# Decayed linear attention and two fp32 feed-forward layers on one core: preparing four instead of two weight pairs of the second layer in the first layer's middle blocks, and four instead of six in its last block

## The chip, the cores and the metric

One core of one Trainium2 chip runs the whole program. The metric is the device time of one execution in microseconds (us), as the median of several runs. A change of this kernel under 0.2% (2.3 us) can't be told from no change.

## The reference

```python
# attention: B, H, S, D = 4, 8, 768, 64
for t in range(S):
    state = gamma * state + outer(k[t], v[t])        # per batch and head
    y[t] = (1/sqrt(D)) * q[t] @ state
x = y.transpose(0, 2, 1, 3).reshape(3072, 512)
# first layer, w_in 512 x 2048, w_out 2048 x 512
h = x @ w_in;  x = max(0.01*h, h) @ w_out
# second layer, the same shapes
h = x @ w_in;  out = (h * cos(h)) @ w_out
```

All of it is in fp32.

## The kernel before

**Precision.** An fp32 operand is split into a high part, rounded to TensorE's fp32r format, and a low part, the remainder. `mm3` (L364 to L366) makes one product of three matmuls: high by high, low by high, high by low. Every operand needs a cast (ScalarE, called ACT in the profile) and a subtraction (VectorE, called DVE, or GpSimd, called POOL).

**Stages.** The 3072 tokens are six blocks of 512. In the first layer the 2048 inner columns are 16 tiles of 128, one iteration each: `gemm1` (12 matmuls into a PSUM tile `hp`), the leaky activation on ACT (L562), the cast of its result `g` (ACT, L570), the low part of `g` (DVE, L574, in `low_g`), and `gemm2_a` (12 matmuls into four banks `acc`) two iterations later. The attention of the next block is done in slots between these: per unit of 128 tokens and four heads the keys and queries are split (`prep_qk`: casts L454 and L458 on ACT, subtractions L459 on DVE and L462 on POOL), then come the scores on TensorE (PE) with the mask on DVE (L491), and for two units at a time the products with the values (L504 to L519) and their evacuation (L530 and L539 on DVE, L541 on ACT, L542 on POOL). The last block has no attention beside it.

**Second layer.** It starts when the first has ended, and multiplies pairs of 256 x 256 blocks by Strassen's scheme in seven products (`product`, "P1" to "P7"). Its weights must be prepared ahead: `w_out` tile by tile (`half`, L650), 16 halves, and `w_in` two tiles at a time (`pair_at`, L665), eight pairs. The inputs of the first two blocks are prepared too (`xprep`, L300). Whatever is prepared goes to DRAM (`w2d`, `w2i`) and is loaded later.

**What a half and a pair are.** The weights come as 64-bit words. One tile goes through these steps: `fetch2` (L250), a DMA on SyncE's queue (SP) into the raw buffer; `exponent` (L121 and L123), two ACT instructions; `clamp`, `fraction` and `top_bits` (L126, L129, L134) on DVE; `round_up` (L139) on POOL; a cast (L271) on ACT; a low part (L278) on POOL or DVE; and the sending of both. A pair does the first steps for two tiles t1 and t2, splits three parts in 512 columns and one in 256, and forms four sums of 256 columns on DVE (`pair_sums`, L288). The raw buffer in the middle blocks is one, `cbuf[0:2]`, so the next fetch there waits for the round_up before it. The last block has its own pool with three buffers each (`last_pairs`, L701).

**What sets the order.** Everything is written in program order, and each engine and each DMA queue works in order. `Agenda` holds lists of steps under numbers called moments; `tick` (L834) runs one moment per half iteration, once after `gemm1` and once after the activation. Moment 0 is iteration 4 of the third block; the last block has the moments 88 (LAST) to 119. `half` and `pair` put their steps at m plus fixed offsets and advance m by 4 and 11; `last_pairs` puts its six pairs at 88, 92, ... 108. A send that is told to wait goes out at the next `flush` (L238), one moment later. `stage` (L102) gives four rotating buffers `o`, which the evacuations of a finished block (L776 and L778) use as well.

Of the kernel before, what the change touches and what calls it, by code (L numbers as in the profile page):

```python
# [28 lines left out]
NF = DFF // P  # L29
# [52 lines left out]
def body(ctx: ExitStack, tc: tile.TileContext, att, w1, w2, tab, out):  # L82
    nc = tc.nc
# [18 lines left out]
    def stage(tag="o"):  # L102
        return tmp.tile([P, BLK], F32, tag=tag, name=tag, bufs=4 if tag == "o" else 2)
# [107 lines left out]
    w2i = [dpool.tile([P, WIN], F32, name=f"w2i{p}") for p in range(NF // 2)]  # L211
# [31 lines left out]
    def send(out, in_, wait):  # L243
        if wait:
            late.append((out, in_))
        else:
            nc.sync.dma_start(out=out, in_=in_)

    def fetch2(raw, f, part):
        nc.sync.dma_start(out=raw, in_=w2[f, :, part * 512 : part * 512 + 512].bitcast(I32))  # L250

    def rounding(raw, t):

        def words():
            return raw().rearrange("p (n t) -> p n t", t=2)

        return (
            lambda: exponent(words(), t()),
            lambda: (clamp(t()), fraction(t()), top_bits(words(), t())),
            lambda: round_up(words(), t()),  # L260
        )

    def parts(t, dst, lo, eng, keep, out, wait=True):


        o = []

        def high():
            n = t().shape[-1]
            o.append(out(n) if out else dst()[:, :n])  # L270
            nc.scalar.copy(out=o[0].bitcast(F32R), in_=t().bitcast(F32))  # L271
            if out:
                send(dst[:, lo : lo + n], o[0], wait)

        def low():
            n = t().shape[-1]
            w = (out(n) if keep else t().bitcast(F32)) if out else dst()[:, n:]
            eng.tensor_tensor(out=w.bitcast(F32R), in0=t().bitcast(F32), in1=o[0].bitcast(F32), op=ALU.subtract)  # L278
            if out:
                send(dst[:, lo + n : lo + 2 * n], w, wait)  # L280

        return high, low
# [7 lines left out]
    def pair_sums(t1, t2):  # L290
        a11, a12, a21, a22 = t1[:, :256], t1[:, 256:], t2[:, :256], t2[:, 256:]
        sub2(a22, a21, a22, ALU.add)
        sub2(a21, a11, a21)
        sub2(a11, a22, a11)
        sub2(a12, a12, a11)

    def done(*what):
        return lambda: made.add(what)
# [260 lines left out]
    class Leaky:  # L559
        def begin(self, hp):  # L560
            t = stage("t")
            nc.scalar.activation(out=t, in_=hp, func=AF.Prelu, alpha=0.01)  # L562
            return (t,)
# [13 lines left out]
    with tc.manual_schedule():  # L577

        with ExitStack() as pctx, ExitStack() as actx:
# [57 lines left out]
            agenda = Agenda()  # L637
            START, LAST = 4, 2 * (NF * (NB - 3) - 4)
            m, turn = 0, 0

            def own(i):
                return lambda: cbuf[:, i, :]
# [7 lines left out]
            def half(f):  # L650
                nonlocal m, turn
                t = own(2 + turn % 2)
                turn += 1
                first, mid, last = rounding(raw2, t)
                high, low = parts(t, w2d[f], 0, nc.gpsimd, False, ostage)
                for i, step in enumerate((begin(f, 1), int, first, mid, last, high, low)):
                    agenda.put(m + i, step)
                agenda.put(m + 6, done("w", f))
                m += 4

            def late_fn(fn):
                first = []
                return lambda: first[0] if first else first.append(fn()) or first[0]

            def pair_at(agenda, b, p, t1, t2, raws, fetches, times, lows, out, out2):  # L665
                r1, r2 = (rounding(raw, t) for raw, t in zip(raws, (t1, t2)))
                g1 = parts(t1, w2i[p], 0, lows[0], True, out)
                both = late_fn(partial(out, 512))
                halves = iter(range(2))

                def half_out(n):
                    return both()[:, next(halves) * 256 :][:, :256]

                g4 = parts(lambda: t2()[:, 256:], w2i[p], 3072, nc.vector, True, half_out)
                g2 = parts(t1, w2i[p], 1024, lows[1], False, out2)
                g3 = parts(t2, w2i[p], 2048, lows[2], False, out2)
                steps = (
                    fetches[0], *r1, fetches[1], *r2, *g1, *g4, lambda: pair_sums(t1(), t2()),
                    g2[0], g3[0], g2[1], g3[1],
                )  # L680
                for at, step in sorted(zip(times, steps), key=lambda x: x[0]):
                    agenda.put(b + at, step)
                agenda.put(b + max(times), done("p", p))

            def pair(p):
                nonlocal m, turn
                t1, t2 = own(2 + turn % 2), own(3 - turn % 2)
                fetches = [begin(2 * p + i, 0) for i in range(2)]
                times = (0, 2, 3, 4, 4, 6, 7, 8, 5, 6, 9, 10, 10, 11, 11, 12, 12)
                pair_at(agenda, m, p, t1, t2, (raw2, raw2), fetches, times, (nc.gpsimd, nc.gpsimd, nc.vector), ostage, ostage)  # L690
                m += 11

            for f in range(8):
                half(f)
            pair(0)
            for f in range(8, NF):
                half(f)
            pair(1)
            xprep(agenda, max(m + 3, LAST + 5), 0, nc.gpsimd)

            def last_pairs(ppool):  # L701
                def room(tag, n, dt, bufs):
                    return ppool.tile([P, n], dt, tag=tag, name=tag, bufs=bufs)

                def pout(n):
                    return room("po", 512, F32, 3)[:, :n]

                for i, p in enumerate(range(2, NF // 2)):
                    t1, t2 = late_fn(partial(room, "t1", 512, I32, 3)), late_fn(partial(room, "t2", 512, I32, 3))
                    raws = [late_fn(partial(room, "raw", 1024, I32, 3)) for _ in range(2)]  # L710
                    fetches = [lambda raw=raw, f=2 * p + j: fetch2(raw(), f, 0) for j, raw in enumerate(raws)]
                    times = (-2 if i else 0, 2, 3, 4, 1, 4, 5, 6, 5, 6, 7, 8, 8, 9, 9, 10, 10)
                    pair_at(agenda, LAST + 4 * i, p, t1, t2, raws, fetches, times, (nc.gpsimd, nc.gpsimd, nc.vector), pout, ostage)

            PRE = ('0000', '0000', '0101', '0010', '0210', '0100', '0200', '0022', 0)
            SEGMENTS = [(0, 0, SPLIT[0]), (1, 0, SPLIT[1]), (0, SPLIT[0], NF), (1, SPLIT[1], NF)] + [(n, 0, NF) for n in range(2, NB)]
# [191 lines left out]
        def finish_one():  # L908
            h, r, pair = before.pop()
            nc.vector.tensor_tensor(out=r, in0=h, in1=r, op=ALU.mult)  # L910
            return r, pair
# [21 lines left out]
        acct, sum2, g1, g2 = [], {}, {}, {}  # L933
# [66 lines left out]
        for q in range(QUADS):  # L1000
# [16 lines left out]
            a, b, c, d = (bpool.tile([P, BLK], F32, tag=x, name=x, bufs=2) for x in "abcd")  # L1017
# [28 lines left out]
        last = finish_one()  # L1046
# [37 lines left out]
```

## Time and profile before

| | before |
|---|---|
| median of 3 runs | 1166.15 us (1165.49 to 1167.23) |
| the profiled execution | 1162.35 us |
| its span | 1160.4 us |
| PE busy | 1123.9 us (97%) |
| DVE busy | 843.1 us (73%) |
| ACT busy | 525.7 us (45%) |
| POOL busy | 318.6 us (27%) |

The span runs from the first to the last instruction of the profiled execution. PE is the engine that is nearly always busy, so the time is that of its matmuls and of what it waits for. The shares are means over stages: in a stretch where another engine is busy nearly all the time, PE may wait there.

### The profile page before, as it was taken

The numbers are of one execution on the slowest core, as the hardware profiler recorded it, in microseconds if no ns is written. First come the engines' busy times: TensorE is split into PE (matmuls) and PEld (weight loads), VectorE is DVE, ScalarE is ACT, GpSimd is POOL, SyncE is SP. The second block draws the span as 40 slices with busy tenths as digits, with TensorE's granted clock in tenths as the row PEclk, the third lists the DMA queues.
The fourth block names the chain that finished last, engine by engine and source line by source line (L and its number), as shares of the span: only waits on it lengthen the run. The fifth ranks groups of instructions, "written<-read, shape, count | busy, mean of one in ns | idle before, by whom it ended". The sixth has DMA issues, their size and how long they took to land.

```text
span 1160.4 us, 15609 instructions
## 1 busy us (share of the span) xinstructions
PE 1123.9 (97%) x5584; PEld 926.5 (80%) x5584; DVE 843.1 (73%) x1299; ACT 525.7 (45%) x954; POOL 318.6 (27%) x288
## 2 busy tenths in 40 slices
PE   6989989999999999999998899999999999999998
PEld 5768778888888888888876668888888888888886
DVE  7899886345455565544599798788798897877875
ACT  5556653233344444443445355444455443444432
POOL 5687773132333444432366300000000000000000
PEclk9999999999999999999999999999999999999999
DMA  9906412222334433432669456549547457333311
GB/s 341 325 5 213 164 54 92 70 77 98 126 122 145 144 129 118 162 111 88 209 228 373 164 181 210 198 167 346 188 151 242 166 216 255 127 136 136 121 79 73
DMA packets 73804, 190.12 MB, mean 164 GB/s; under 512 B 8192, under 2 KB 12416, under 8 KB 73728
## 3 DMA queue, kind: packets, MB, share of 16 engines
q1 hardware_dynamic: 73584, 188.88, 46.6%
q8 instruction: 44, 0.72, 0.3%
q14 instruction: 32, 0.26, 0.1%
q10 hardware_dynamic: 144, 0.26, 0.1%
HBM read 136.68 MB, written 52.43 MB: 163 GB/s over the span
## 4 chain that ended last, share of the span: by engine, by line
PE 75%; DVE 14%; DMA 4%; issue 2%; POOL 2%; ACT 2%; SPq 0%; ACTq 0%; POOLq 0%; DVEq 0%
PE hp L364 9%; PE hp L366 9%; PE hp L365 9%; PE acc L364 9%; PE acc L365 9%; PE acc L366 9%; PE attB L364 4%; PE attB L365 4%; PE attB L366 4%; PE attA L364 2%; PE attA L366 2%; PE attA L365 2%; DVE cbuf L129 2%; DVE g L574 2%; DVE cbuf L134 2%
## 5 line engine op out<-in xcount | busy, mean ns | idle before, releaser
L366 PE MATMUL acc<-g,w 128*128 128x512 f32 x384 | 151.8, 395 | 7.9 <-DVE g L574 7.8
L364 PE MATMUL acc<-g,w 128*128 128x512 f32 x384 | 153.1, 399 | 2.0 <-DVE o L778 1.5
L364 PE MATMUL hp<-b,w 128*128 128x512 f32 x384 | 150.6, 392 | 4.4 <-ACT t L562 3.2
L366 PE MATMUL hp<-b,w 128*128 128x512 f32 x384 | 150.1, 391 | 1.1 <-POOL b L542 1.0
L365 PE MATMUL acc<-g,w 128*128 128x512 f32 x384 | 151.0, 393 | 0.0
L365 PE MATMUL hp<-b,w 128*128 128x512 f32 x384 | 149.6, 390 | 0.0
L922 ACT ACTIVATE r<-r,bias 128x512 f32<-128x512 f32 x96 | 69.6, 725 | 88.0 <-DVE r L921 88.0
L574 DVE TENSOR_TENSOR g<-t,g 128x512 fp32r<-128x512 f32 x91 | 89.4, 983 | 18.2 <-ACT g L570 17.6
L366 PEld LDWEIGHTS acc<-g,w 128*128 128x128 f32 x384 | 72.9, 190 | 25.8 <-DVE g L574 9.9
L364 PE MATMUL hp<-w,b 128*128 128x512 f32 x224 | 87.5, 391 | 2.9 <-ACT a L1018 2.2
L364 PEld LDWEIGHTS hp<-b,w 128*128 128x128 f32 x384 | 72.3, 188 | 20.8 <-ACT t L562 4.1
L364 PEld LDWEIGHTS acc<-g,w 128*128 128x128 f32 x384 | 72.8, 190 | 18.3 <-DVE o L778 1.9
L365 PE MATMUL hp<-w,b 128*128 128x512 f32 x224 | 87.2, 389 | 0.0
L366 PE MATMUL hp<-w,b 128*128 128x512 f32 x224 | 87.1, 389 | 0.0
L570 ACT CAST g<-t 128x512 fp32r<-128x512 f32 x96 | 59.4, 619 | 61.0 <-PE acc L366 60.3
L366 PEld LDWEIGHTS hp<-b,w 128*128 128x128 f32 x384 | 72.1, 188 | 17.5 <-POOL b L542 2.4
L365 PEld LDWEIGHTS acc<-g,w 128*128 128x128 f32 x384 | 72.8, 190 | 14.0
L365 PEld LDWEIGHTS hp<-b,w 128*128 128x128 f32 x384 | 72.1, 188 | 14.3
L365 PE MATMUL acc<-w,g 128*128 128x512 f32 x192 | 75.0, 391 | 1.1 <-DVE g L574 1.0
L366 PE MATMUL acc<-w,g 128*128 128x512 f32 x192 | 74.7, 389 | 0.0
L364 PE MATMUL acc<-w,g 128*128 128x512 f32 x192 | 74.7, 389 | 0.0
L562 ACT ACTIVATE t<-hp 128x512 f32<-128x512 f32 x96 | 56.9, 593 | 32.9 <-PE hp L366 30.4
(196 smaller groups left out, 2521.0 us busy)
## 6 DMA issues: line engine op xcount, KB each, us to landing
b<-w2i SPq DMA_DIRECT2D x60, 512.0 KB, 5.7
w<-w SPq DMA_DIRECT2D x32, 512.0 KB, 7.4
raw<-att SPq DMA_DIRECT2D x32, 512.0 KB, 4.2
w<-w2d SPq DMA_DIRECT2D x32, 512.0 KB, 7.7
w<-xq SPq DMA_DIRECT2D x28, 512.0 KB, 5.3
cbuf<-w SPq DMA_DIRECT2D x20, 512.0 KB, 4.0
xq<-o SPq DMA_DIRECT2D x40, 256.0 KB, 2.3
w<-att SPq DMA_DIRECT2D x14, 512.0 KB, 7.4
```

Of the source, the lines that this page charges most:

```text
L129: nc.vector.tensor_scalar(out=t, in0=t, scalar1=3, scalar2=LOW_BITS, op0=ALU.logical_shift_left, op1=ALU.bitwise_and)
L134: nc.vector.scalar_tensor_tensor(out=t, in0=raw[:, :, 1], scalar=SIGN_TOP, in1=t, op0=ALU.bitwise_and, op1=ALU.bitwise_or)
L364: nc.tensor.matmul(o, sh, mh, start=start, stop=False)
L365: nc.tensor.matmul(o, sl, mh, start=False, stop=False)
L366: nc.tensor.matmul(o, sh, ml, start=False, stop=stop)
L562: nc.scalar.activation(out=t, in_=hp, func=AF.Prelu, alpha=0.01)
L570: nc.scalar.copy(out=pair[:, 0], in_=g)
L574: eng.tensor_tensor(out=pair[:, 1], in0=g, in1=pair[:, 0].bitcast(F32), op=ALU.subtract)
L922: nc.scalar.activation(out=r, in_=r, func=AF.Sin, bias=bias[:, 1:2], scale=1.0)
```

## The change

A half takes three moments of the timetable instead of four: the three DVE steps and the round_up stand in one moment. A pair in the middle blocks takes nine instead of eleven, and writes the low parts of its second and third part to `o` buffers instead of over t1 and t2 (`keep`). Four halves and a pair take turns, four times, which uses 84 moments; before, eight halves and a pair came twice and used 86. So the pairs 2 and 3 move from the last block to the middle blocks; the last block's remaining four stand six moments apart instead of four. The number of instructions on DVE, ACT and POOL for a pair stays the same.

```diff
@@ half
-                for i, step in enumerate((begin(f, 1), int, first, mid, last, high, low)):
+                for i, step in zip((0, 2, 3, 3, 4, 5), (begin(f, 1), first, mid, last, high, low)):
                     agenda.put(m + i, step)
-                agenda.put(m + 6, done("w", f))
-                m += 4
+                agenda.put(m + 5, done("w", f))
+                m += 3
@@ pair_at
-            def pair_at(agenda, b, p, t1, t2, raws, fetches, times, lows, out, out2):
+            def pair_at(agenda, b, p, t1, t2, raws, fetches, times, lows, out, out2, keep=False):
...
-                g2 = parts(t1, w2i[p], 1024, lows[1], False, out2)
-                g3 = parts(t2, w2i[p], 2048, lows[2], False, out2)
+                g2 = parts(t1, w2i[p], 1024, lows[1], keep, out2)
+                g3 = parts(t2, w2i[p], 2048, lows[2], keep, out2)
@@ pair
-                times = (0, 2, 3, 4, 4, 6, 7, 8, 5, 6, 9, 10, 10, 11, 11, 12, 12)
-                pair_at(agenda, m, p, t1, t2, (raw2, raw2), fetches, times, (nc.gpsimd, nc.gpsimd, nc.vector), ostage, ostage)
-                m += 11
+                times = (0, 2, 3, 3, 3, 5, 6, 6, 4, 5, 7, 8, 8, 9, 9, 10, 10)
+                pair_at(agenda, m, p, t1, t2, (raw2, raw2), fetches, times, (nc.gpsimd, nc.gpsimd, nc.vector), ostage, ostage, True)
+                m += 9
-            for f in range(8):
-                half(f)
-            pair(0)
-            for f in range(8, NF):
-                half(f)
-            pair(1)
+            OWN = 4
+            for p in range(OWN):
+                for f in range(4 * p, 4 * p + 4):
+                    half(f)
+                pair(p)
@@ last_pairs
-                for i, p in enumerate(range(2, NF // 2)):
+                for i, p in enumerate(range(OWN, NF // 2)):
...
-                    pair_at(agenda, LAST + 4 * i, p, t1, t2, raws, fetches, times, (nc.gpsimd, nc.gpsimd, nc.vector), pout, ostage)
+                    pair_at(agenda, LAST + 6 * i, p, t1, t2, raws, fetches, times, (nc.gpsimd, nc.gpsimd, nc.vector), pout, ostage)
```

**ACT in a middle block.** The rows begin with the cast of two attention products (L541). kh and qbd are the split keys and queries of the next unit, `cbuf` the weight words, `o` their high part. Before, in any of the later middle blocks:

```order
L541 CAST b_3195<-xs 128x2x128 x2
L562 ACTIVATE t<-hp 128x512
L454 CAST kh<-raw 128x256
L458 CAST qbd<-raw 64x2x128 x2
L271 CAST o<-cbuf 128x512
L570 CAST g<-t 128x512
L121 ACTIVATE cbuf<-cbuf 128x512
L123 ACTIVATE cbuf<-cbuf 128x512
L562 ACTIVATE t<-hp 128x512
L570 CAST g<-t 128x512
L454 CAST kh<-raw 128x256
L458 CAST qbd<-raw 64x2x128 x2
```

In the change, in one of the cycles whose products come just ahead of an exponent:

```order
L541 CAST b_2318<-xs 128x2x128 x2
L121 ACTIVATE cbuf<-cbuf 128x512
L123 ACTIVATE cbuf<-cbuf 128x512
L562 ACTIVATE t<-hp 128x512
L454 CAST kh<-raw 128x256
L458 CAST qbd<-raw 64x2x128 x2
L570 CAST g<-t 128x512
L271 CAST o<-cbuf 128x512
L562 ACTIVATE t<-hp 128x512
L121 ACTIVATE cbuf<-cbuf 128x512
L123 ACTIVATE cbuf<-cbuf 128x512
L570 CAST g<-t 128x512
```

The exponent (L121, L123) of a third half now stands ahead of the first unit's casts (L454, L458), and another stands ahead of the second unit's, which follow directly behind the last row shown.

**DVE in the last block.** Each row L574 is the low part of one iteration's g; the t_ tiles are the words of the pairs, `po` is an output buffer. Before, between two rows L574:

```order
L574 TENSOR_TENSOR g<-t,g 128x512
L126 TENSOR_SCALAR t_5312<-t_5312 128x512
L129 TENSOR_SCALAR t_5312<-t_5312 128x512
L134 SCALAR_TENSOR_TENSOR t_5312<-raw,t_5312 128x512
L278 TENSOR_TENSOR po<-t_5251,po 128x256
L288 TENSOR_TENSOR t_5251<-t_5251 128x256
L288 TENSOR_TENSOR t_5251<-t_5192,t_5251 128x256
L288 TENSOR_TENSOR t_5192<-t_5251,t_5192 128x256
L288 TENSOR_TENSOR t_5192<-t_5192 128x256
L574 TENSOR_TENSOR g<-t,g 128x512
```

In the change, between three rows L574 at the like place:

```order
L574 TENSOR_TENSOR g<-t,g 128x512
L126 TENSOR_SCALAR t_5098<-t_5098 128x512
L129 TENSOR_SCALAR t_5098<-t_5098 128x512
L134 SCALAR_TENSOR_TENSOR t_5098<-raw,t_5098 128x512
L574 TENSOR_TENSOR g<-t,g 128x512
L278 TENSOR_TENSOR po<-t_5098,po 128x256
L288 TENSOR_TENSOR t_5098<-t_5098 128x256
L288 TENSOR_TENSOR t_5098<-t_5061,t_5098 128x256
L288 TENSOR_TENSOR t_5061<-t_5098,t_5061 128x256
L288 TENSOR_TENSOR t_5061<-t_5061 128x256
L574 TENSOR_TENSOR g<-t,g 128x512
```

Where the word steps of the next pair (L126 to L134) and the part with its four sums (L278, L288) stood together ahead of one low part of g, each of the two now has an iteration of its own.

## Rows read from the trace of the kernel before

**Rows 1.** Busy time in stretches: PE, PEld, DVE, ACT, POOL, clock, DMA share, GB/s.

```profile
275.90:545.80 269.90, 269.90 (x1500) 227.08 (x1499) 145.92 (x252) 115.23 (x233) 109.60 (x101) 1.00 0.37 125
...
597.40:650.27 52.87, 45.04 (x179) 35.56 (x179) 50.15 (x56) 27.50 (x52) 35.19 (x23) 0.94 0.77 285
...
659.40:710.00 50.60, 47.69 (x203) 37.75 (x204) 45.10 (x71) 25.48 (x41) 0.00 (x0) 1.00 0.48 161
```

**Rows 2.** Timeline of PE: start, length (us), line, matmul, idle before and its releaser.

```profile
550.67 0.39 PE L364 MATMUL hp<-b,w 128*128 128x512 f32 x1
...
553.39 0.39 PE L364 MATMUL acc<-g,w 128*128 128x512 f32 x1
...
598.26 0.50 PE L366 MATMUL acc<-g,w 128*128 128x512 f32 x1 [0.74 <-DVE g L574]
...
650.27 0.39 PE L364 MATMUL hp<-w,b 128*128 128x512 f32 x1
...
659.40 0.50 PE L364 MATMUL hp<-w,b 128*128 128x512 f32 x1 [2.17 <-ACT a L1018]
...
688.10 0.50 PE L364 MATMUL hp<-w,b 128*128 128x512 f32 x1 [0.77 <-DVE c L903]
...
696.27 0.50 PE L364 MATMUL attA<-w,b 128*128 128x512 f32 x1 [1.16 <-ACT a L1018]
```

**Rows 3.** DVE by line and form, 563 to 660 us: count, busy us, mean ns.

```profile
L574 DVE TENSOR_TENSOR g<-t,g 128x512 fp32r<-128x512 f32 x15 | 16.8, 1123 | 0.0
L288 DVE TENSOR_TENSOR t<-t 128x256 f32<-128x256 f32 x12 | 10.0, 832 | 0.4
L288 DVE TENSOR_TENSOR t<-t,t 128x256 f32<-128x256 f32 x12 | 9.9, 825 | 0.8
L288 DVE TENSOR_TENSOR cbuf<-cbuf 128x512 f32<-128x512 f32 x8 | 9.8, 1231 | 0.0
L126 DVE TENSOR_SCALAR t<-t 128x512 f32<-128x512 f32 x11 | 9.0, 818 | 0.0
L134 DVE SCALAR_TENSOR_TENSOR t<-raw,t 128x512 int32<-128x512 int32 x11 | 8.7, 794 | 0.4
L129 DVE TENSOR_SCALAR t<-t 128x512 int32<-128x512 int32 x11 | 8.6, 782 | 0.4
L278 DVE TENSOR_TENSOR t<-t,o 128x512 fp32r<-128x512 f32 x6 | 7.1, 1180 | 0.6 <-ACT o L271 0.6
L278 DVE TENSOR_TENSOR po<-t,po 128x256 fp32r<-128x256 f32 x6 | 6.9, 1157 | 1.6 <-ACT po L271 1.6
```

**Rows 4.** Timeline of ACT at the second layer’s first product.

```profile
658.76 0.59 ACT L1018 COPY a<-hp 128x512 f32<-128x512 f32 x1 [4.35 <-DMA w2i<-t]
```

**Rows 5.** Timeline of the SP queue in a middle block: two successive fetches.

```profile
382.43 0.33 SPq L250 DMA_DIRECT2D cbuf<-w  x1
...
392.21 0.33 SPq L250 DMA_DIRECT2D cbuf<-w  x1
```

**Rows 6.** Timeline of ACT in the same stretch: exponent, leaky activation.

```profile
386.50 0.67 ACT L121 ACTIVATE cbuf<-cbuf 128x512 f32<-128x512 f32 x1 [2.92 <-DMA cbuf<-w]
...
387.64 0.57 ACT L562 ACTIVATE t<-hp 128x512 f32<-128x512 f32 x1
```

**Rows 7.** Timeline of DVE in the same stretch: subtractions, last word step, subtractions.

```profile
381.46 2.11 DVE L459 TENSOR_TENSOR qbd<-raw,qbd 64x256 fp32r<-64x256 f32 x2 [0.97 <-ACT qbd L458]
...
388.45 0.69 DVE L134 SCALAR_TENSOR_TENSOR cbuf<-cbuf 128x512 int32<-128x512 int32 x1
...
389.51 1.51 DVE L459 TENSOR_TENSOR qbd<-raw,qbd 64x256 fp32r<-64x256 f32 x2 [0.36 <-ACT qbd L458]
```

**Rows 8.** Timeline of POOL in the same stretch: the rounding addition.

```profile
390.70 1.48 POOL L139 TENSOR_TENSOR cbuf<-cbuf 128x512 int32<-128x512 int32 x1
```

**Rows 9.** Timeline of PE in the same stretch: first matmul of two score groups.

```profile
386.02 0.28 PE L364 MATMUL attA<-qbd,kh 128*128 128x256 f32 x1
...
394.92 0.28 PE L364 MATMUL attB<-qbd,kh 128*128 128x256 f32 x1
```

## The prediction

> **What bounds the kernel now.** I began with the page's busy shares: PE 97%, the next engine DVE 73%. A share that high says only that what can be won lies in the few places where PE waits, so I then cut the span into stretches [rows 1]. In the middle blocks, from the first fetch of the second layer's weights at 275.9 us on, PE is busy for all of 269.90 us while DVE has 145.92 and POOL 109.60: PE sets the pace and everyone else has room. In the second half of the last block it is the reverse: PE 45.04 of 52.87 us, DVE 50.15, and the granted clock 0.94 instead of 1.00. In the start of the second layer PE has 47.69 of 50.60. Third, the timeline of PE tells where exactly [rows 2]. One `gemm1` of 12 matmuls takes 553.39 − 550.67 = 2.72 us, so an iteration of the last block is 5.44 us and its 16 are 87.0. They last from 550.67 to 650.27, 99.6 us: **12.6 us are lost**, idle time and the slower clock after it together. The first stall, at 598.26, waits for DVE's L574, the low part of g. A second kind comes at 659.40: 2.17 us for ACT's copy `a` (L1018), which itself waited 4.35 us for a transfer w2i<-t, the last pair's send [rows 4]. Three more stalls, of 0.77 to 1.16 us, follow between 688.10 and 696.27, some 2.9 us.
>
> Fourth, the groups of DVE in that block say why [rows 3]. The word steps of one tile are 0.818 + 0.782 + 0.794 = 2.39 us, the 256-column low part 1.16, four sums 4 × 0.83 = 3.31, the 512-column low part 1.18. A pair is 2 × 2.39 + 1.16 + 3.31 + 1.18 = 10.4 us of DVE. A low part of g is 1.12. Two iterations, one pair, are then 10.4 + 2.2 = 12.7 us against PE's 10.9, and 14.3 where `xprep` puts 8 subtractions of 1.23 us into 24 moments beside them. DVE can't keep up, falls back, and PE runs out of g.
>
> **The change part by part.**
>
> *Last block, two pairs fewer and six moments apart.* Three iterations now hold one pair, three low parts of g and, in the busiest part, 2.5 us of `xprep`: 10.4 + 3.4 + 2.5 = 16.3 us against PE's 16.3. That just fits if DVE's instructions stay as long as they are. But the sum alone doesn't tell whether the low part of g comes in time. For that I add up the order of DVE (the rows of both kernels are with the change). Before, from one L574 to the next, the stretches ahead of the first stall are 3.5, 8.0, 7.2 and 10.4 us where PE needs 5.44 each: DVE is 9.3 us late when PE first stalls. In the change the stretches are 3.5, 5.6, 7.2, 6.0, 5.6, 4.7, 3.5: at most 2.5 us late, and back to none after the sixth. So I expect none of the stalls on L574, and with them the slow clock goes, since in that block the granted clock only fell behind such waits. **−12.6 us.** Bounds: if DVE's lateness is spread otherwise than the mean durations say (ACT waits for the sums, then DVE for ACT), a third could stay, −8; it can't be over 12.6.
>
> *Start of the second layer.* The last pair starts at moment 106 instead of 108, two moments or 2.7 us earlier, and doesn't lag. Its send lands well ahead of the copy `a`. **−2.2 us.** What comes late next is DVE's row of additions in the first two groups, the three stalls behind 688 us. DVE starts them earlier than before by more than PE gains, so they may shrink; I count them as unchanged, with −2.9 as the bound.
>
> *Middle blocks, two pairs more.* The instructions themselves are hidden. Two pairs are 21 us of DVE at the last block's durations, and DVE idles for 124 us of that stretch; POOL idles for 160. The two kept low parts are the same subtractions with another output; only the four buffers `o` are used seven times per pair instead of five, and the sends behind them leave a moment later, ahead of the evacuations of a finished block (no cost taken; up to 2 us where three evacuations could wait for them).
>
> What can cost is order. A half has three moments now, and its phase against the attention's cycle of eight moments changes from one cycle to the next, where it stood still before. The casts of the next unit's keys and queries have little room: in a middle block DVE's subtractions for the first unit end at 381.46 + 2.11 = 383.57 and its scores start at 386.02, 2.45 us later; for the second unit 391.02 and 394.92, 3.90 us [rows 7, 9]. In three of the cycles the change puts an exponent ahead of both units' casts (the second ACT block shown with the change). First unit: the exponent's two instructions push the casts by 387.64 − 386.50 = 1.14 us [rows 6], less than 2.45, no stall. The subtractions then end at 384.7. The word steps take until 2.64 us after an exponent's start (386.50 to the end of 388.45 + 0.69), less the exponent's own 0.67, 2.0; round_up 1.48 [rows 6 to 8]. The fetch behind it therefore goes out at 388.2, and lands as before 386.50 − 382.43 = 4.07 us later [rows 5, 6], at 392.2. The second unit's casts stand behind this exponent: from there to the end of the subtractions before it was 391.02 − 386.50 = 4.5 us, less half a us for the activation that no longer stands between, so 396.2 to 396.7 where the scores want them at 394.92. With the shorter word steps that nothing on POOL hinders it would be near 395.5. That is 0.6 to 1.8 us late; I take the middle, 1.2 us a cycle, three times: **+3.6 us.** Bounds: 0, if the phases slip a little, to 3 times 3.2 = 9.6, where the word steps meet POOL.
>
> On the last bound a rule speaks against the change. In these rows two equal pairs of subtractions took 2.11 and 1.51 us [rows 7], and the one beside POOL's work is the longer. The Trainium skill ("SBUF — State Buffer", section "Who interferes with whom") says that a VectorE instruction with two SBUF inputs and a GpSimd instruction that reads SBUF exclude each other, for the whole instruction. The trace agrees in kind. By that rule each of the three late subtractions could lose another POOL instruction, 1.48 us, and the middle term would be 8.0 instead of 3.6. By the rows alone it stays at 3.6, since POOL has done its round_up by then.
>
> *The sum.* −12.6 − 2.2 + 3.6 = −11.2 us. The profiled execution took 1162.35 us, its span is 1160.4: by the sum 1151.2. The median of the runs is 3.8 us above that execution, and I carry the difference over: **1155.0 us.**
>
> **Rivals.**
>
> 1. *All of it is hidden.* The middle blocks cost nothing, and the second layer's first stalls go as well: −12.6 − 2.2 − 2.9 = −17.7, 1148.5. For it: PE shows no wait at all in 269.90 us [rows 1]. Against: the room ahead of the scores is only 2.45 us.
>
> 2. *The last block gains half.* ACT works in order too: its casts of the parts wait for the four sums, and g's cast stands behind them. If that chain and not DVE's load is what makes g late, fewer pairs help only in part: −6.3 of 12.6, −2.2, +3.6, so −4.9, 1161.2. For it: by the sum of 16.3 against 16.3 us next to nothing is free in DVE's busiest part. Against: DVE had next to no idle time in that stretch [rows 1], so its load came first.
>
> 3. *Slower: the one raw buffer becomes the pace of the middle blocks.* From fetch to fetch is a loop of transfer, exponent, word steps and round_up, 392.21 − 382.43 = 9.78 us [rows 5]. 88 moments pass from 275.9 to 553.4, 3.15 us each, so the 21 moments of four halves and a pair, with six fetches, are 66 us, 11.0 per loop. While the loop is shorter, lateness is made good at the next pair; beyond 11.0, each us more costs one in all of 24 loops, 24 us. At 11.6 it has eaten the gain. If loops run at 12.0 because each of their instructions queues behind attention work, +24 − 14.8 = +9.2, 1175.4. For it: all four engines of the loop work in order and wait for attention. Against: 9.78 was measured with such waits in it.
>
> 4. *No change:* the middle term sits near its upper bound and the last block gains least, −8 − 2.2 + 9.6 = −0.6, 1165.5.
>
> That the pairs don't move at all is excluded: the order of DVE shows four pairs in the last block.
>
> **How the numbers follow.** Chances: the forecast (gains of 6.5 to 15 us) 0.62, rival 1 0.15, rival 2 0.10, rival 3 0.08, rival 4 0.05. A difference within 2.3 us (0.2%) counts as none. Faster is the forecast with rivals 1 and 2, 0.87; the same is rival 4, 0.05; slower is rival 3, 0.08. The likeliest gives 1155.0. The range goes from 1148.5, where rival 1 puts the time, to 1162.0, just past rival 2; outside are rivals 3 and 4 and the far tail of rival 1, some 0.17.
>
> **What would show it.** Right: sixteen iterations of the last block in 87 to 89 us, no wait for L574 above half a us there, a granted clock of 1.00 in it, no wait of `a` for w2i. In the middle blocks a few waits of PE's scores for L459 of around one us, in the cycles named, and ACT's exponents waiting for cbuf<-w at most some 3 us. Wrong: waits for L574 that stay, with ACT waiting for L288 ahead of them (rival 2); fetches over 11 us apart again and again, and PE waits in nearly every cycle (rival 3); or no PE wait at all between 276 and 550 us (rival 1).

## The result, and the profile after

| | before | after |
|---|---|---|
| median | 1166.14 us (1165.49 to 1167.23, 4 runs) | 1152.78 us (1152.53 to 1153.05, 4 runs) |
| the profiled execution | 1162.35 us | 1152.64 us |
| its span | 1160.4 us | 1150.5 us |
| PE busy | 1123.9 us | 1122.2 us |
| DVE busy | 843.1 us | 830.7 us |

The change is faster: ratio 0.9885, 95% interval 0.9870 to 0.9901. The forecast was 1155.0. Times below are medians too; one execution of the changed kernel took 2897.8 us, in its repeat further below, and is not counted there.

The windows that answer to [rows 1] (same columns: PE, PEld, DVE, ACT, POOL, clock, DMA share, GB/s) are the middle blocks, the second half of the last block, and the start of the second layer from P5 on:

```profile
278.10:548.00 269.90, 268.29 (x1487) 224.93 (x1487) 156.04 (x276) 122.54 (x249) 121.06 (x110) 1.00 0.44 147
...
599.25:642.77 43.52, 43.52 (x194) 36.05 (x192) 37.39 (x42) 21.32 (x40) 27.35 (x19) 1.00 0.77 281
...
649.57:700.00 50.43, 47.51 (x204) 37.55 (x203) 44.37 (x70) 25.49 (x41) 0.00 (x0) 1.00 0.46 162
```

The last block has turned round: its second half takes 43.5 us instead of 52.9, PE is busy for all of it, and DVE is idle for 6.1 us of it where it was for 2.7 in a longer stretch. In the middle blocks, where PE never waited, it is now idle for some 1.6 us. The timeline of PE that answers to [rows 2] gives the places: four waits in the middle, then the starts of the last block, the second layer and P5 (the fourth product that the second layer makes), then three stalls. (Lines behind the preparation of the middle blocks' pairs are one lower than before: L777 was L778.)

```profile
320.80 0.38 PE L366 MATMUL attB<-qbd,kh 128*128 128x256 f32 x1 [0.24 <-DVE qbd L459]
...
398.43 0.38 PE L366 MATMUL attB<-qbd,kh 128*128 128x256 f32 x1 [0.24 <-DVE qbd L459]
...
475.67 0.39 PE L366 MATMUL attB<-qbd,kh 128*128 128x256 f32 x1 [0.31 <-DVE qbd L459]
...
477.92 0.50 PE L364 MATMUL acc<-g,w 128*128 128x512 f32 x1 [0.82 <-DVE o L777]
...
555.73 0.39 PE L364 MATMUL hp<-b,w 128*128 128x512 f32 x1
...
642.77 0.39 PE L364 MATMUL hp<-w,b 128*128 128x512 f32 x1
...
649.57 0.39 PE L364 MATMUL hp<-w,b 128*128 128x512 f32 x1
...
678.16 0.50 PE L364 MATMUL hp<-w,b 128*128 128x512 f32 x1 [0.78 <-DVE c L902]
...
681.03 0.50 PE L365 MATMUL acc<-w,g 128*128 128x512 f32 x1 [0.98 <-DVE g L574]
...
686.34 0.50 PE L364 MATMUL attA<-w,b 128*128 128x512 f32 x1 [1.16 <-ACT a L1017]
```

With the starts in [rows 2] the difference of the spans adds up:

| stretch | before | after | difference |
|---|---|---|---|
| up to the last block | 550.67 | 555.73 | +5.06 |
| the last block's 16 iterations | 99.60 | 87.04 | −12.56 |
| from there to P5 | 9.13 | 6.80 | −2.33 |
| the rest | | | −0.07 |
| span | 1160.4 | 1150.5 | −9.9 |

Of the +5.06, 2.7 us are the middle blocks: PE falls back by 0.5 at each of the first three waits and by 1.1 at the fourth. (A wait is counted from the end of the matmul before; on time, the next one starts ahead of that end, so PE loses more than the wait shows.) The other 2.4 lie ahead of 162 us, where the two kernels are the same; 1.6 of them are one stretch at half the clock, in the last section. A second profile of the change (after_again, the repeat further below) has other waits, 0.60 us at 398.24 and 0.81 at 477.50, and the same cost: from the same matmul near 162 us to the last block's start the change takes 390.9 us in both, the kernel before 388.2.

DVE's groups from 563 to 650 us, in the columns of [rows 3], show that there are eight word steps of each kind and four parts where there were eleven and six, and that the means have moved both ways.

```profile
L574 DVE TENSOR_TENSOR g<-t,g 128x512 fp32r<-128x512 f32 x15 | 15.7, 1053 | 1.4 <-ACT g L570 1.4
L288 DVE TENSOR_TENSOR t<-t,t 128x256 f32<-128x256 f32 x8 | 7.8, 979 | 0.9 <-DVE t L288 0.5
L288 DVE TENSOR_TENSOR cbuf<-cbuf 128x512 f32<-128x512 f32 x8 | 7.7, 961 | 0.0
L288 DVE TENSOR_TENSOR t<-t 128x256 f32<-128x256 f32 x8 | 7.5, 934 | 0.3
L126 DVE TENSOR_SCALAR t<-t 128x512 f32<-128x512 f32 x8 | 5.6, 695 | 0.0
L134 DVE SCALAR_TENSOR_TENSOR t<-raw,t 128x512 int32<-128x512 int32 x8 | 5.5, 693 | 0.3
L278 DVE TENSOR_TENSOR po<-t,po 128x256 fp32r<-128x256 f32 x4 | 5.4, 1349 | 5.4 <-ACT po L271 5.4
L278 DVE TENSOR_TENSOR t<-t,o 128x512 fp32r<-128x512 f32 x4 | 4.8, 1190 | 2.8 <-ACT o L271 2.8
L129 DVE TENSOR_SCALAR t<-t 128x512 int32<-128x512 int32 x8 | 4.4, 549 | 0.3
```

The word steps of a tile fell from 2.39 to 1.94 us; the sums became longer (from 0.83 to 0.93 and 0.98), and so did the 256-column low part (from 1.16 to 1.35). A pair is 10.2 us of DVE, next to no less than the 10.4 of before. The wait for ACT's g (1.4 us) lies at 643.68, behind the block. How near DVE still comes shows where its low part of g is ready last against PE's need, DVE first and then PE:

```profile
638.39 0.68 DVE L574 TENSOR_TENSOR g<-t,g 128x512 fp32r<-128x512 f32 x1
```

```profile
640.50 0.39 PE L366 MATMUL acc<-g,w 128*128 128x512 f32 x1
```

Between the end of the one and the start of the other are 1.43 us. The copy `a` of the second layer's first product, which had waited 4.35 us for a transfer [rows 4], waits for PE's own product:

```profile
644.37 0.59 ACT L1017 COPY a<-hp 128x512 f32<-128x512 f32 x1 [0.73 <-PE hp L366]
```

### The profile page after: what moved, and what is told of

Read it like the earlier page. It is cut to its first block, busy times and chain, and to the rows that moved or that the text cites. A ratio compares the mean times of both kernels' runs of the same rounds, so it can differ in the third digit from the quotient of the medians.

```text
span 1150.5 us, 15592 instructions
## 1 busy us (share of the span) xinstructions
PE 1122.2 (98%) x5584; PEld 926.4 (81%) x5584; DVE 830.7 (72%) x1299; ACT 525.0 (46%) x954; POOL 316.2 (27%) x288
## 4 chain that ended last, share of the span: by engine, by line
PE 78%; DVE 12%; DMA 4%; POOL 2%; issue 2%; ACT 2%; SPq 0%; ACTq 0%; DVEq 0%; POOLq 0%
PE hp L366 10%; PE hp L364 10%; PE hp L365 10%; PE acc L364 9%; PE acc L365 9%; PE acc L366 9%; PE attB L366 4%; PE attB L364 4%; PE attB L365 4%; PE attA L364 2%; PE attA L366 2%; PE attA L365 2%; DVE cbuf L129 2%; DVE cbuf L134 2%; DVE g L574 2%
## 5 line engine op out<-in xcount | busy, mean ns | idle before, releaser
L574 DVE TENSOR_TENSOR g<-t,g 128x512 fp32r<-128x512 f32 x91 | 86.6, 952 | 16.5 <-ACT g L570 15.9
L365 PEld LDWEIGHTS hp<-b,w 128*128 128x128 f32 x384 | 72.4, 189 | 14.5
L459 DVE TENSOR_TENSOR qbd<-raw,qbd 64x256 fp32r<-64x256 f32 x64 | 52.4, 818 | 38.5 <-ACT qbd L458 37.4
```

What stands on the lines that cost most here:

```text
L365: nc.tensor.matmul(o, sl, mh, start=False, stop=False)
L459: nc.vector.tensor_tensor(out=ql[rows, :, cols], in0=rq[rows], in1=qh[rows, :, cols].bitcast(F32), op=ALU.subtract)
L574: eng.tensor_tensor(out=pair[:, 1], in0=g, in1=pair[:, 0].bitcast(F32), op=ALU.subtract)
```

## The experiments

Ratios are against the kernel before, run on the same chip beside them (medians 1164.0 to 1165.2), and edits are against the changed kernel.

### What the last block gains from: two pairs fewer, or six moments apart

Two kernels take one half of the change each. In the first, the tighter timetable prepares two pairs in the middle as before, so that the last block has its six:

```diff
-            OWN = 4
+            OWN = 2
-                for f in range(4 * p, 4 * p + 4):
+                for f in range(8 * p, 8 * p + 8):
...
-                    pair_at(agenda, LAST + 6 * i, ...)
+                    pair_at(agenda, LAST + 4 * i, ...)
```

> The changed timetable of halves and pairs in the middle blocks, but only two pairs there, and six in the last block, four moments apart as before. If the gain is all in the last block (fewer pairs, DVE in time): the last block loses its 12.6 us again and the second layer's start its 2.3, and the middle blocks lose what the three marked waits cost in the changed kernel, here two cycles of 0.5 us, one of them with an evacuation's 1.1: some 1168 us, 2 us above before. If the tighter timetable itself gains something: well under 1166. If the middle term is nothing: 1166.

1169.62, ratio 1.0038 (1.0024 to 1.0052), a little above what was expected. PE waits four times in the middle blocks, 2.5 us together, and the last block takes 100.84 us (557.06 to 657.90). Both kinds of [rows 2]'s stalls are back in it and behind it:

```profile
647.36 0.79 PE L366 MATMUL acc<-g,w 128*128 128x512 f32 x1 [3.85 <-DVE g L574]
...
666.54 0.50 PE L364 MATMUL hp<-w,b 128*128 128x512 f32 x1 [1.68 <-ACT a L1017]
```

So the tighter timetable by itself is a cost: from 162 us to the last block this kernel takes 4.1 us longer than before, and the block 1.2. The second kernel keeps four pairs in the last block, but four moments apart:

```diff
-                    pair_at(agenda, LAST + 6 * i, ...)
+                    pair_at(agenda, LAST + 4 * i, ...)
```

> The changed kernel with the last block's four pairs four moments apart instead of six. If DVE's lateness decides, its order is that of before up to the fourth pair, so the first stalls of before come back, 1.0, 1.3 and perhaps 2.0 us: 2.4 to 4.3 us above the changed kernel, 1155 to 1157 us. If only the number of pairs decides, not their spacing: 1152.8.

1155.33, ratio 0.9917 (0.9902 to 0.9932). The block takes 90.31 us, 3.27 more than in the change:

```profile
602.02 0.50 PE L366 MATMUL acc<-g,w 128*128 128x512 f32 x1 [1.16 <-DVE g L574]
```

A second stall of 1.08 us follows at 614.27. Of the 12.6 us, 9.3 come from the two pairs that leave and 3.3 from the distance of those that stay, when the two steps are taken in this order.

The distance was tried once more with five pairs in the last block, five moments apart, and three in the middle:

```diff
-            OWN = 4
-            for p in range(OWN):
-                for f in range(4 * p, 4 * p + 4):
+            OWN = 3
+            for p, (lo, hi) in enumerate(((0, 5), (5, 10), (10, 16))):
+                for f in range(lo, hi):
...
-                    pair_at(agenda, LAST + 6 * i, ...)
+                    pair_at(agenda, LAST + 5 * i, ...)
```

> Three pairs in the middle blocks, five in the last, five moments apart. Adding up DVE's order with the mean durations of before gives at most 9 us of lateness up to the fourth pair and 11 at the fifth, where 9 is where PE first stalled: about 2 us of stall at the end of the block, 1154 to 1156 us. If the loss goes with the number of pairs in a straight line, 7 us of the 14.9 come back: 1160.

A miss: 1161.77 (1158.98 to 1164.11), ratio 0.9974 (0.9961 to 0.9987).

```profile
640.39 0.50 PE L366 MATMUL acc<-g,w 128*128 128x512 f32 x1 [0.87 <-DVE g L574]
...
647.54 0.50 PE L366 MATMUL acc<-g,w 128*128 128x512 f32 x1 [1.42 <-DVE g L574]
...
654.67 0.50 PE L364 MATMUL hp<-w,b 128*128 128x512 f32 x1 [3.21 <-ACT a L1017]
```

The expectation had counted DVE's load and forgotten the end: five pairs five moments apart start the last one at moment 108, as before. The copy `a` waits 4.3 us for w2i<-t again, and from the second layer's start to P5 it is 11.88 us instead of 6.80. The block itself takes 88.30 us, 1.3 more than in the change, and behind 655.57 us 3.4 us follow at the lower clock, which cost 1.7.

### Is it DVE's load?

Rival 2 had ACT's chain make g late. The trace of before speaks against it already. Ahead of its last stall in the block, at 640.79, ACT's cast and DVE's low part of the same g are:

```profile
631.15 0.61 ACT L570 CAST g<-t 128x512 fp32r<-128x512 f32 x1
```

```profile
640.06 0.68 DVE L574 TENSOR_TENSOR g<-t,g 128x512 fp32r<-128x512 f32 x1
```

The cast had ended 8.3 us before DVE came to it; at the five stalls it was 2.7 to 10.3 us. To test DVE's load by itself, 68 additions of 128 columns on a tile that nothing else uses were put on DVE in the last block. No instruction of ACT is added.

```diff
+                extra = ppool.tile([P, 128], F32, tag="extra", name="extra", bufs=1)
+                agenda.put(LAST + 3, lambda: nc.vector.memset(extra, 0.0))
+                for i in range(17):
+                    for _ in range(4):
+                        agenda.put(LAST + 4 + i, lambda: nc.vector.tensor_tensor(out=extra, in0=extra, in1=extra, op=ALU.add))
```

> The changed kernel with 68 additional DVE additions of 128 columns on a tile of their own in the last block, four a moment over 17 moments; nobody waits for them. If it is DVE's load that made g late, some 20 us more of it (68 times about 0.3 us) bring stalls on the low part of g back, 8 to 12 us: 1161 to 1165 us. If g is late through ACT's waits for the sums (the chain of two engines and not the load), little changes: under 1155.

1165.89, ratio 1.0008 (0.9999 to 1.0018): as slow as before, and slower than expected. The additions' group, and the stretch of the last block in the columns of [rows 1]:

```profile
L711 DVE TENSOR_TENSOR extra<-extra 128x128 f32<-128x128 f32 x68 | 37.2, 548 | 1.9
```

```profile
556.05:657.60 101.55, 91.00 (x385) 73.27 (x384) 87.05 (x142) 43.25 (x79) 42.85 (x30) 0.97 0.57 188
```

The additions took 37.2 us, and the block 101.55, 14.5 more than in the change: about the 12.6 that the change took away, with the same stalls on L574. More time on DVE alone brings the loss back, and with the casts above rival 2 falls as the first cause. At the longest stall the cast had ended 11.1 us before DVE came to it. Not all of this time is work, though: 50 of the additions took 0.28 to 0.29 us and 18, all beside an instruction of POOL, 1.23 to 1.40 (see the last section). The longest stall is also the plainest picture of what a wait leaves behind. PE's timeline and then the window behind the wait (PE busy, clock, DMA share, GB/s):

```profile
609.29 0.80 PE L366 MATMUL acc<-g,w 128*128 128x512 f32 x1 [4.99 <-DVE g L574]
609.88 0.63 PE L364 MATMUL acc<-g,w 128*128 128x512 f32 x1
610.31 0.63 PE L365 MATMUL acc<-g,w 128*128 128x512 f32 x1
```

```profile
609.29:613.30 4.01, 4.01 (x10) 0.50 0.37 142
```

Ten matmuls start 0.43 us apart where [rows 2] has 12 in 2.72, 0.227 each: the lower of the two clocks, 1.2 GHz, and some 2 us lost on top of the 4.99.

### Are the middle blocks' waits a matter of phase?

The prediction laid the waits to cycles in which an exponent stands ahead of both units' casts. If so, moving the whole timetable by some moments against the attention must change them, at no cost elsewhere. By the order of ACT there are three such cycles in the change, one if everything starts two moments later, and one, the last, if it starts seven later:

```diff
-            m, turn = 0, 0
+            m, turn = 2, 0
```

> The changed kernel with the whole timetable of the middle blocks begun two moments later. The exponents then stand ahead of both units' casts in one full cycle instead of three, and no evacuation of a finished block shares a cycle with that. If PE's waits in the middle blocks come from this place in ACT's order: 0.5 us are left of the 2.7, 1150 to 1151.5 us. If they come from the load of DVE and POOL, which doesn't change: 1152.8.

1150.49, ratio 0.9881 (0.9866 to 0.9896). Two waits are left, 0.24 at 346.48 and 0.34 at 477.55. Then seven moments:

```diff
-            m, turn = 0, 0
+            m, turn = 7, 0
```

> The same, begun seven moments later: one full cycle with the exponents ahead of both units' casts (the last one of the middle blocks), evacuations in other cycles. By the place in ACT's order 0.5 to 1 us of the 2.7 are left, 1150.5 to 1152 us; by load alone 1152.8. The last pair then ends seven moments nearer to the last block's work, which might cost up to 1 us at its beginning.

1149.40, ratio 0.9871 (0.9854 to 0.9887), one wait of 0.20: 1 us less than expected. This kernel was run once more, beside the changed kernel itself, to see whether so little holds:

> The changed kernel as it is, beside the shifted one on the same chip: 1152 to 1153 us.

> The timetable begun seven moments later, beside the unshifted one on the same chip. If the three waits for the casts and the one for the evacuation are what it saves: 2.2 to 3.5 us under the changed kernel, 1149 to 1150.5. If the earlier difference was one of the chips: the same as the changed kernel.

The changed kernel: 1151.97 (1150.85 to 1152.14, three executions), ratio 0.9885 (0.9864 to 0.9905). Seven moments later: 1150.22 (1150.01 to 1150.40), ratio 0.9874 (0.9860 to 0.9889). Beside each other on one chip that is 1.8 us less, where 2.2 to 3.5 were expected; against the first runs of the change the first runs of this kernel are 3.4 us lower. The intervals of the ratios overlap, the ranges of the runs don't. By the medians alone 1.8 us is less than the 2.3 that count as a change; what bears it are the traces. It is the fastest version found. The same work of the middle blocks, first in the change, then in this kernel:

```profile
283.00:555.70 272.70, 271.09 (x1500) 227.28 (x1499) 154.15 (x271) 121.94 (x246) 118.87 (x106) 1.00 0.45 147
```

```profile
283.00:553.20 270.20, 270.17 (x1500) 227.16 (x1499) 150.04 (x262) 118.61 (x240) 114.28 (x103) 1.00 0.41 136
```

It takes 2.5 us less, and PE's waits are gone. From 162 us to the last block the change takes 390.9 us, the kernel two moments later 389.6, the one seven moments later 388.6 and 388.5 in its two profiles, before 388.2. So nearly all of the 2.7 us of the middle blocks are the phase, not the work.

### The kept low parts

One part of the edit keeps t1 and t2 and puts two low parts into `o` buffers. Without it:

```diff
-                pair_at(agenda, m, p, ..., ostage, ostage, True)
+                pair_at(agenda, m, p, ..., ostage, ostage, False)
```

> The changed kernel, but the pairs of the middle blocks write the low parts of the second and third part over t1 and t2 again, as before. The next half's exponent writes t1 and then waits for the send of that low part, 2 to 4 us more than now, behind each of three pairs. If that wait reaches PE (through the casts behind it on ACT): 1 to 3 us above the changed kernel, 1154 to 1156. If the room hides it: 1152.8.

1152.27, ratio 0.9893 (0.9879 to 0.9908), the same as the change. ACT's next exponents wait twice, 4.4 us together, for the buffer that the low parts are sent from, but PE doesn't wait for it. Keeping them isn't what the gain needs.

### How near is rival 3?

Rival 3 had the loop through the one raw buffer set the pace. Each of its 24 rounds is made longer here by one POOL addition behind the round_up (the words it writes are not used):

```diff
-            lambda: round_up(words(), t()),
+            (lambda: (round_up(words(), t()), nc.gpsimd.tensor_tensor(out=words()[:, :, 0], in0=t(), in1=words()[:, :, 0], op=ALU.add))) if more else (lambda: round_up(words(), t())),
...
```

> The changed kernel with one more addition on POOL behind each round_up of the middle blocks, into the raw buffer's low words, which nobody reads again; only the next fetch waits for it, 1.5 us more in each of 24 loops. By the account of three marked cycles their waits grow by 1.5 us each and some other cycles begin to wait: 1156 to 1160 us. If the loop is the pace of the middle blocks already (rival 3, 11.0 us each against 9.8 + 1.5): 7 us or more above, over 1160. If there is room everywhere: 1153 to 1154.

1171.25, ratio 1.0060 (1.0043 to 1.0077): 18.5 us lost, far past what the account of three cycles gave and well inside what was set for rival 3 (over 1160). The waits of the whole span (us in total, times, longest), first of the change, then of this kernel:

```profile
ACT cbuf L121 <- DMA cbuf<-w: 44.4, 17, 3.5
```

```profile
ACT cbuf L121 <- DMA cbuf<-w: 70.3, 20, 4.7
```

PE then waits for what stands behind those exponents on ACT, the casts of the queries, and for the evacuation:

```profile
381.61 0.50 PE L364 MATMUL acc<-g,w 128*128 128x512 f32 x1 [2.01 <-DVE o L777]
...
407.05 0.39 PE L364 MATMUL attB<-qbd,kh 128*128 128x256 f32 x1 [2.52 <-ACT qbd L458]
```

The same work as in the two windows above takes 291.00 us here, with 12.7 of idle and the rest of the loss in slower matmuls:

```profile
283.00:574.00 291.00, 278.25 (x1499) 229.95 (x1498) 157.62 (x271) 121.97 (x246) 150.47 (x130) 0.98 0.42 136
```

POOL has 31.6 us more to do in this stretch, which could be the cause instead of the loop. So 24 additional POOL instructions were put where no fetch waits for them, as repeats of low parts (a half's low part then has the high part taken off twice):

```diff
...
-            eng.tensor_tensor(out=w.bitcast(F32R), ..., op=ALU.subtract)
+            for _ in range(times):
+                eng.tensor_tensor(out=w.bitcast(F32R), ..., op=ALU.subtract)
...
-                high, low = parts(t, w2d[f], 0, nc.gpsimd, False, ostage)
+                high, low = parts(t, w2d[f], 0, nc.gpsimd, False, ostage, times=2)
...
-                g1 = parts(t1, w2i[p], 0, lows[0], True, out)
+                g1 = parts(t1, w2i[p], 0, lows[0], True, out, times=3 if keep else 1)
```

> The control for the lengthened loop: the same 24 additional POOL instructions of 1.3 to 1.5 us in the middle blocks, but behind the low parts (those of the halves and the first part of the pairs, done twice and three times), where no fetch waits for them. The low parts of w_out are falsified by it. If the 18.5 us of the lengthened loop came from the loop from fetch to fetch: at most 2 us above the changed kernel, 1153 to 1155 us. If they came from POOL's load (the key subtractions behind it in POOL's order): well over 1160.

1154.87, ratio 0.9912 (0.9897 to 0.9927): 2.1 us more than the first runs of the change, 2.9 more than its repeat on this chip, of the 18.5. So POOL's load by itself is not the cause; the rest goes with the place behind the round_up, which the loop runs through. (That place also stands ahead of the next key subtractions on POOL. In the lengthened kernel PE's longest waits are not for those, but for ACT's casts and the evacuation.) PE's waits here are on late subtractions, such as (L460 is L459 of the others)

```profile
399.94 0.39 PE L367 MATMUL attB<-qbd,kh 128*128 128x256 f32 x1 [0.61 <-DVE qbd L460]
```

## Why the prediction was right, and where it was not

**Last block: −12.6 forecast, −12.56 measured.** The reason held as well: no wait for L574, a granted clock of 1.00, 87.04 us where 87 to 89 were to be seen. The deciding step was to add up DVE's order; the experiments give 9.3 of it to the pairs that left and 3.3 to the distance, and the additions on DVE alone undo it. Two sizes were off without harm. The summed lateness, at most 2.5 us where before stalled at 9.3 (its own stretches give 2.6, back to none after the seventh), left nearly 7 us of room at the worst place; the trace shows the 1.43 above. And the sum of 16.3 against 16.3 us is 15.3 with the means after: a pair is nearly as long as it was, and the 1 us comes from `xprep` (1.9 instead of 2.5), the low parts of g (3.2 instead of 3.4) and the pair (10.2 instead of 10.4). That the gain came out to a tenth is in part the cap: with no stall left, 12.6 is all there is.

**Second layer's start: −2.2 forecast, −2.33 measured.** That it was the last pair's send is shown from the other side too, by the kernels whose last pair starts at moment 108. The three stalls behind it "may shrink", the text said, and counted them as unchanged. They are unchanged: 0.78, 0.98 and 1.16 us. DVE's additions did not start earlier against PE, as the text had it: the one ahead of the first stall starts 0.74 us before it in both kernels (677.42 to 678.16, and 687.36 to 688.10). What they hang on was not tried.

**Middle blocks: +3.6 forecast, +2.7 measured, and made up otherwise.** The term is mis-sized in two steps that partly cancel, and that it came so near is in part luck. The three cycles were the right ones (waits at 320.80, 398.43 and 475.67), but each costs 0.5 us in this profile, not 1.2. (The order of ACT before, shown with the change, holds up to 402 us; from 428 on the cast of the words and the exponent stand earlier. In both, one exponent lies between the two units' casts and none ahead of the first's.) The cycle that the prediction worked out can be followed in the trace, on SP, ACT and DVE in turn:

```profile
312.95 0.33 SPq L250 DMA_DIRECT2D cbuf<-w  x1
```

```profile
316.86 0.67 ACT L121 ACTIVATE cbuf<-cbuf 128x512 f32<-128x512 f32 x1 [2.78 <-DMA cbuf<-w]
...
318.79 0.83 ACT L458 CAST qbd<-raw 64x256 fp32r<-64x256 f32 x2
```

```profile
319.23 0.76 DVE L459 TENSOR_TENSOR qbd<-raw,qbd 64x256 fp32r<-64x256 f32 x1 [6.36 <-ACT qbd L458]
320.02 0.73 DVE L459 TENSOR_TENSOR qbd<-raw,qbd 64x256 fp32r<-64x256 f32 x1
```

The cycle lies 74.91 us ahead of the one in the sum. The fetch was to go out at 313.3 and did at 312.95; the exponent was to start at 317.3 and did at 316.86; the subtractions were to end at 321.3 to 321.8 and did at 320.75. That is 0.4 us early from the first step on and another 0.1 to 0.6 in the casts. And what is late hits less: the scores' first two matmuls (at 160 and 280 ns past 320 us) use the high part of the queries, which the cast alone gives; only the third uses the low part. The wait is therefore a quarter of a microsecond in the trace. The step that failed is the one that measured the subtractions' end against the start of the scores.

On the rule of the Trainium skill ("SBUF — State Buffer", section "Who interferes with whom"), by which the term would have been 8.0: the late subtractions took 0.76 and 0.73 us, as in the shorter pair in [rows 7], and did not lose another POOL instruction of 1.48 us, since the next round_up begins at 322.47. That does not speak against the rule. The prediction took the shorter pair for one without POOL; but POOL works beside both pairs, from 381.11 and from 389.25 us on, and beside this one too (L462 and L477, 318.97 to 320.47). The three of the 64 subtractions with no POOL instruction beside them took 0.42 us each. So the late subtractions were lengthened too, by an amount that the rows already held. With 24 more POOL instructions in these blocks the kernel lost 2 to 3 us, a tenth of a microsecond each.

The other 1.1 us is the wait at 477.92 for an evacuation, which had been priced at nothing, with up to 2 us if buffers `o` were short. It isn't the buffers. DVE's order at that place:

```profile
474.11 1.50 DVE L459 TENSOR_TENSOR qbd<-raw,qbd 64x256 fp32r<-64x256 f32 x2 [6.45 <-ACT qbd L458]
475.65 0.43 DVE L126 TENSOR_SCALAR cbuf<-cbuf 128x512 f32<-128x512 f32 x1
...
477.18 1.28 DVE L777 COPY o<-acc 128x512 f32<-128x512 f32 x2
```

Late casts hold the subtractions, the word steps follow at once, and the copies out of `acc` stand behind them. DVE had stood idle for 6.45 us before. So the same late cast is paid for a second time, by another customer. That fits the kernels that start two and seven moments later, where the evacuations fall into other cycles and this wait is 0.34 us and gone.

**From the profile to the median: +3.8 us carried over, 0.1 measured.** This is the largest error. It hides 1.5 us by which the profiled pair of executions gained less than the sum (9.7 instead of 11.2), so that 1155.0 is only 2.2 us off. Before's profiled execution was at the fast end of its kind: 18 runs of that kernel in one session range from 1163.40 to 1166.97, the two at the bottom with a mean clock of 0.997, the four above 1166 with 0.990 to 0.994. After's runs lie within 0.5 us of each other, at 0.996 to 0.997. The median gained 13.4 where the profiled pair shows 9.7. Of these 3.7 us, 2.4 can be seen: it is the stretch ahead of 162 us, where the kernels are the same and before's profiled execution happened to be quicker, 1.6 of it because the clock did not fall there. The other 1.3 are not explained. They may belong to stalls that are gone, since after some of them the clock falls, and not in each execution; that is argued, not shown by a run of its own.

**The rivals.** Rival 1 did not come true as put (the three stalls stay), but its half in the middle blocks is nearly reached by starting the timetable seven moments later. Rival 2 is excluded by the casts in before's trace and by the additions on DVE. Rival 3 is real and was nearer than its law said: from 9.78 us, one instruction of 1.3 us more (31.6 us / 24) makes 11.1, which by 24 us for each us beyond 11.0 costs 2 or 3; it cost 18.5. The 9.78 were one pair of fetches. In the change 24 fetches go out from 278.12 to 533.26, 7.5 to 15.7 us apart and 11.1 in the mean, which is the timetable's own pace; with the longer loop they are 12.0 apart in the mean. So of the 1.3 us added to a round some 0.95 come out as a longer round: in the mean there was little room left, whatever one short round says.

## What to carry to other kernels

Where an engine is behind for a whole stage, add up its instructions between two successive deliveries in program order and compare each sum with the pace of the engine it feeds; here that told rightly that the stalls would go. Take the room that is left from the trace after: the sum had nearly 7 us, the trace 1.43. When work is moved under a stage that has room, its cost is the order, not the work: try the same timetable at a few offsets against the loop it runs beside (worth 1.8 to 3.4 us here), and follow a late instruction to all that stands behind it on its engine. And don't carry the offset between one profiled execution and the median over to another kernel; look first for what that execution was spared, in code that is the same.

## What the runs showed of the hardware

The same wait does not always bring the same clock. PE waits 2.08 us at 158.11 in the change and 2.09 at 157.37 before, in code that is the same. The window behind it, in the change and then before (PE busy, clock, DMA share, GB/s):

```profile
158.80:161.90 3.10, 3.10 (x9) 0.50 0.00 0
```

```profile
158.10:161.20 3.10, 3.10 (x15) 1.00 0.00 0
```

Nine matmuls instead of fifteen: 1.6 us that no line of the change accounts for. The same drop is in the profiles of six of these kernels (eight profiles) and is missing in those of five.

What a DVE instruction costs here goes with whether POOL works at the same time. In the last block before, an instruction of POOL and the word step on DVE beside it are:

```profile
602.44 1.75 POOL L278 TENSOR_TENSOR po<-t,po 128x512 fp32r<-128x512 f32 x1
```

```profile
602.95 1.52 DVE L126 TENSOR_SCALAR t<-t 128x512 f32<-128x512 f32 x1
```

The same step takes 0.42 us at 598.12. Of the 93 DVE instructions that start in that block, 35 took over 1.3 times as long as the shortest of their form, and every one of them overlaps an instruction of POOL. Together the 93 took 86.9 us, where at the shortest of each form they would take 49.9; in the change it is 66.5 and 41.1 (74 instructions, 25 of them longer). So of the 20 us that left DVE in this block some 9 are work and 12 are such lengthening. That POOL is the cause is read from the overlaps: a kernel that takes POOL's work and not DVE's out of the last block was not run.

The additions of 128 columns tell the same: 279 ns at the least and 1403 at the most, 548 in the mean. The expectation for them went by about 0.3 us, near the shortest, and was wrong by nearly half.
